# Local attention in blocks of 32 queries with 44 keys, its softmax in single operations, and coarse queries averaged on TensorE

## The chip, the cores and the metric

The kernel runs on one core of one Trainium2 chip. The metric is device microseconds of one launch: 507.03 us is the median of three runs before the change (505.02 to 508.1). One execution was taken by the hardware profiler; every row shown below is of that one.

## The reference, cut to what matters

There are 2 batches, 8 heads, 576 positions and a head width of 64. For each batch and head the kernel computes two attentions and adds them; the sum, transposed to 1152 tokens by 512, goes through two feed-forward layers (512 to 2048 to 512).

```python
# coarse attention: means of 4 positions, 144 queries by 144 keys
q_d, k_d, v_d = (t.reshape(B, H, 144, 4, D).mean(axis=3) for t in (q, k, v))
out_up = np.repeat(softmax(scale * q_d @ k_d.T) @ v_d, 4, axis=2)
# local attention: a key counts only where |query - key| < 4
scores = np.where(abs(pos[:, None] - pos[None, :]) < 4, scale * q @ k.T, -1e9)
out_local = softmax(scores) @ v
x = out_up + out_local          # -> (1152, 512)
# layer 1: h = x @ w_in;  g = P(h) / Q(h), polynomials;  x = g @ w_out
# layer 2: h = x @ w_in2; g = h * tanh(softplus(h));     out = g @ w_out2
```

The weights arrive as 64-bit floats and are turned into pairs of 32-bit values on ScalarE and VectorE. Each product of the layers is three matmuls (high by high, high by low, low by high).

## The kernel before, in words

**Planner.** The body adds tasks (`add`), each with its engines, the time it is believed to take on each, a priority, the tasks it follows and the buffers it takes. `Plan.run` walks a model of the time and emits the tasks of each of five queues (TensorE, ScalarE, VectorE, GpSimd, SyncE) in the order in which they start in that model; on the chip every queue then runs in that fixed order. A task that names two engines goes to the one that the model finds sooner, with a preference for the first named. Where TensorE has nothing ready before the model's 450 us it emits a filler matmul (`warm0`, `warm`, lines 442 and 445), whose result nobody reads.

**Attention units.** Sixteen units each take one batch, one pair of heads and 256 positions (4 windows of 64 queries); two mixed units take the last 64 positions of all four pairs of heads. So there are 18. Two heads lie on partitions 0 to 63 and 64 to 127. `prep` (eight times, once for each batch and pair) loads and transposes the keys and makes the coarse keys `kd` and coarse values `vd`. A unit then goes through these steps:

- `qload` (line 564) loads the queries, `vload` (line 578) the values of the 4 windows, 80 keys each, in two loads, one for each head.
- `pe_a` transposes the queries with 2 transposes (line 465) into a PSUM half bank `half`. From it `red` (line 599, VectorE) sums groups of four queries, `qscale` (line 616, GpSimd) scales the sums, and `qcopy` (line 609, ScalarE) copies the scaled queries to `qT`.
- `pe_b` writes a mask of -1e9 with 2 matmuls (line 638), adds the scores of 4 windows by 80 keys for each head (line 644), then the coarse scores by 144 keys (line 650). An f32 matmul stands as two instructions in the trace, so the 8 of line 644 are 16.
- `mx` takes the row maxima (lines 662 and 663, VectorE). `ex` runs four exponentials of 80 columns, each with its own bias and a read of its row sum (line 669), and one of 144 columns (line 673). `rc` makes the reciprocals of the sums (lines 681 and 684), `ns` scales the local part (line 689, GpSimd) and `npd` the coarse part (line 695, VectorE).
- `pe_d` transposes both parts (lines 707 and 711: 2 and 4 transposes); `copy_pd` (line 723) and `copy_p` (line 728) bring them from PSUM.
- `pe_e` multiplies by the values (lines 744 and 750). `od_c` (763) and `xadd` (770) add both attentions; `xhi` (789) and `xlo` (794) split the sum in two for the layers.

**Layers.** Layer 1 runs first over 6 of its 16 blocks of 128 hidden columns, in token chunks of 256, 256, 256 and 384; chunk c can start only when the units of its tokens are through. So units and layer 1 are interleaved on all engines until all units are done. The rest of layer 1, then layer 2, run in chunks of 384. Lines 1019 and 1167 are the matmuls of layer 1 (line 1019 also the first of layer 2), line 1169 those of the end of layer 2. Lines 899 to 930 turn the weights into pairs, lines 1040 to 1134 are the nonlinear parts.

**PSUM.** Two half banks `half` serve the query transposes and the coarse transposes in turn; scores, transposes `pt` and outputs `po` have one bank each. For the first chunk there is a second slot of each but `po`.

**Loads.** All loads are issued by SyncE in one order; a load that waits for its buffer holds those behind it.

## Time and profile before

| what | before |
|---|---|
| median of 3 runs | 507.03 us (505.02 to 508.1) |
| profiled execution, first to last instruction (span) | 502.4 us |
| median less the profiled span | 4.6 us |
| TensorE matmuls busy | 483.9 us, 96% |
| VectorE busy | 346.9 us, 69% |
| ScalarE busy | 341.7 us, 68% |
| GpSimd busy | 69.4 us, 14% |
| granted TensorE clock | 1.000 over the span |
| DMA | 44119 packets, 46.49 MB, 27568 packets under 512 B |

The profiled execution's own time is known only as its span; what lies around the span is taken as the 4.6 us to the median. PE stands for TensorE, PEld for its weight loads, DVE for VectorE, ACT for ScalarE, POOL for GpSimd and SP for SyncE; a q behind a name is its instruction queue. The busy shares are means over stages: the kernel has a stage with attention, one in which layer 1 runs alone, and one in which layer 2 runs alone.

### The profile page before, as it was taken

How to read it: one execution, taken by the hardware profiler on the slowest of the kernel's cores; microseconds unless marked ns; L12 is line 12 of the kernel's file. 1: busy time of each engine (PE TensorE's matmuls, PEld its weight loads, DVE VectorE, ACT ScalarE, POOL GpSimd, SP SyncE). 2: the span in 40 equal slices, each digit the busy share in tenths (PEclk: the TensorE clock that was granted, in tenths of full speed). 3: DMA queues.
4: the chain of work that ended last, by engine and by line, in shares of the span. 5: the costliest groups of instructions: out<-in, count | busy, mean ns of one | idle time of the engine just before them, and what ended most of it. 6: DMA issues, size and time to landing. Idle time of an engine off the chain costs nothing.

```text
span 502.4 us, 8614 instructions
## 1 busy us (share of the span) xinstructions
PE 483.9 (96%) x3468; PEld 442.0 (88%) x3468; DVE 346.9 (69%) x482; ACT 341.7 (68%) x612; POOL 69.4 (14%) x85
## 2 busy tenths in 40 slices
PE   8989898999999999999999989999999999999996
PEld 4568677899999999998998989899899899988995
DVE  5678888998999987989889999644723613222222
ACT  6699989998999999997999997555621322112210
POOL 3743764132000000000000413000000000000000
PEclk9999999999999999999999999999999999999999
DMA  9979765330245042315024040522400000000111
GB/s 186 208 226 199 205 176 145 105 105 14 87 166 168 2 168 83 90 78 168 2 83 168 8 161 1 167 85 83 168 0 1 0 1 0 1 0 1 63 64 63
DMA packets 44119, 46.49 MB, mean 93 GB/s; under 512 B 27568, under 2 KB 30640, under 8 KB 44080
## 3 DMA queue, kind: packets, MB, share of 16 engines
q1 hardware_dynamic: 44080, 45.95, 31.6%
q8 instruction: 27, 0.44, 0.4%
q14 instruction: 12, 0.10, 0.1%
HBM read 43.58 MB, written 2.36 MB: 91 GB/s over the span
## 4 chain that ended last, share of the span: by engine, by line
PE 45%; ACT 29%; DVE 13%; DMA 6%; issue 4%; SPq 1%; POOL 0%; DVEq 0%; ACTq 0%; POOLq 0%
PE psum L1019 21%; PE psum L1169 19%; ACT L961 4%; ACT raw L906 3%; DMA raw<-in_moe_w_in_dram 2%; ACT wt L899 2%; ACT wrk L1045 2%; PE psum L1167 2%; ACT late_f L1048 2%; ACT wrk L1040 2%; ACT late_f L977 2%; ACT att L669 1%; ACT gg L1134 1%; DMA att<-in_q_dram 1%; DVE wt L913 1%
## 5 line engine op out<-in xcount | busy, mean ns | idle before, releaser
L1019 PE MATMUL psum<-xh,wi 128*128 128x384 f32 (+1 forms) x528 | 132.5, 324 | 0.0
L1019 PEld LDWEIGHTS psum<-xh,wi 128*128 128x128 f32 x528 | 93.5, 188 | 1.2 <-issue 0.8
L1019 PE MATMUL psum<-xl,wi 128*128 128x384 f32 (+1 forms) x264 | 84.5, 320 | 0.0
L1019 PE MATMUL psum<-xh,late_r 128*128 128x384 f32 x288 | 76.7, 335 | 1.3 <-DVE late_f L1063 1.3
L1167 PE MATMUL psum<-gg,wo 128*128 128x384 f32 (+1 forms) x456 | 72.2, 312 | 0.9 <-ACT gg L1134 0.5
L1167 PEld LDWEIGHTS psum<-gg,wo 128*128 128x128 f32 x456 | 68.7, 189 | 2.3 <-ACT gg L1134 1.0
L1019 PEld LDWEIGHTS psum<-xh,late_r 128*128 128x128 f32 x288 | 52.3, 188 | 2.1 <-DVE late_f L1063 1.6
L1169 PE MATMUL psum<-wo,gg 128*128 128x512 f32 x216 | 51.1, 391 | 0.0
L1019 PEld LDWEIGHTS psum<-xl,wi 128*128 128x128 f32 x264 | 49.8, 189 | 0.2
L1019 PE MATMUL psum<-xl,late_r 128*128 128x384 f32 x144 | 48.3, 335 | 0.8 <-POOL xl L1226 0.8
L1169 PEld LDWEIGHTS psum<-wo,gg 128*128 128x128 f32 x216 | 40.4, 188 | 8.1
L1113 ACT ACTIVATE late_f<-psum 128x768 f32<-128x768 f32 (+1 forms) x12 | 9.5, 791 | 55.1 <-PE psum L1019 55.1
L913 DVE SCALAR_TENSOR_TENSOR wt<-wt,raw 128x1024 int32<-128x1024 int32 x32 | 41.7, 1304 | 5.0 <-ACT raw L906 4.1
L1246 DVE TENSOR_TENSOR part<-psum,part 128x512 f32<-128x512 f32 x27 | 18.4, 692 | 35.2 <-PE psum L1169 35.2
L899 ACT ACTIVATE wt<-raw 128x1024 f32<-128x1024 f32 x32 | 36.8, 1150 | 8.2 <-DVE late_r L930 3.8
L906 ACT ACTIVATE raw<-raw 128x1024 int32<-128x1024 uint16 x32 | 37.2, 1162 | 6.3 <-DMA raw<-in_moe_w_out_dram 4.7
L1113 ACT ACTIVATE wrk<-psum 128x768 f32<-128x768 f32 (+1 forms) x13 | 10.3, 790 | 43.2 <-PE psum L1019 43.2
L1226 POOL TENSOR_TENSOR xl<-part,xh 128x768 fp32r<-128x768 f32 x5 | 11.6, 2321 | 176.5 <-ACT xh L1221 176.0
L1139 DVE TENSOR_TENSOR gg<-wrk,gg 128x768 fp32r<-128x768 f32 (+1 forms) x22 | 18.6, 845 | 23.1 <-ACT gg L1113 22.9
L1019 PEld LDWEIGHTS psum<-xl,late_r 128*128 128x128 f32 x144 | 27.0, 188 | 1.4 <-POOL xl L1226 1.1
L1169 PE MATMUL psum<-wo,late_r 128*128 128x512 f32 x108 | 25.7, 391 | 0.0
L1139 DVE TENSOR_TENSOR gg<-late_f,gg 128x768 fp32r<-128x768 f32 (+1 forms) x15 | 15.4, 1024 | 14.4 <-ACT gg L1113 13.9
(135 smaller groups left out, 937.7 us busy)
## 6 DMA issues: line engine op xcount, KB each, us to landing
raw<-in_moe_w_in_dram SPq DMA_DIRECT2D x16, 1024.0 KB, 5.2
raw<-in_moe_w_out_dram SPq DMA_DIRECT2D x16, 1024.0 KB
att<-in_v_dram SPq DMA_DIRECT2D x36, 80.0 KB, 5.0
out_dram<-part SPq DMA_DIRECT2D x9, 256.0 KB, 2.2
att<-in_q_dram SPq DMA_DIRECT2D x16, 128.0 KB, 4.0
att<-in_k_dram SPq DMA_DIRECT2D x6, 288.0 KB, 4.4
att<-in_v_dram SPq DMA_DIRECT2D x6, 256.0 KB, 4.0
wrk<-in_k_dram SPq DMA_DIRECT2D x2, 288.0 KB, 5.8
```

The lines of the kernel that those rows point to most:

```text
L899: nc.scalar.activation(out=t.v, in_=words(r)[:, :, 1].bitcast(F32), func=AF.Prelu if fold else AF.Identity, scale=2.0 ** -112, **({"alpha" ...
L906: nc.scalar.activation(out=words(r)[:, :, 0], in_=r.v.bitcast(U16).rearrange("p (n four) -> p n four", four=4)[:, :, 1], func=AF.Copy, sca ...
L913: nc.vector.scalar_tensor_tensor(out=ti, in0=ti, scalar=3, in1=words(r)[:, :, 0], op0=ALU.logical_shift_left, op1=ALU.bitwise_or)
L961: nc.scalar.preload_act_table_set(name)
L977: nc.scalar.activation(out=st.B(), in_=st.B(), func=AF.Sigmoid, scale=-1.0)
L1019: nc.tensor.matmul(st.h.v[:, i, :T], w.v[:, ww, ks], xx[:, kk, c0:c0 + T], start=(nn == 0 and (st.big or i == 0)), stop=(nn == 3 * KD - 1 ...
L1113: nc.scalar.activation(out=vw(dst), in_=H(), func=AF.Mish)
L1139: ENG[e].tensor_tensor(out=vw(st.gl), in0=vw(st.c), in1=vw(st.gh).bitcast(F32), op=ALU.subtract)
L1167: nc.tensor.matmul(A(d)[:, :T], w.v[:, ww, lo + d * 128:lo + (d + 1) * 128], vw(gg)[:, i, :], start=start, stop=stop)
L1169: nc.tensor.matmul(A(d), vw(gg)[:, i, sl], w.v[:, ww, lo:lo + DM], start=start, stop=stop)
L1226: ENG[e].tensor_tensor(out=xl[xs], in0=pv, in1=xh[xs].bitcast(F32), op=ALU.subtract)
L1246: nc.vector.tensor_tensor(out=pv, in0=acc.v[:, j], in1=pv, op=ALU.add)
```

## The change

The windows of a unit become blocks of 32 queries with 44 keys (`WK` 80 to 44), eight to a unit. Their results lie in a `[128, 4, 44]` array of scores: partition quarters hold head and block, and `SLOT` gives the place of a window.

- `vload` issues four loads of 44 keys in place of two of 80 (eight small ones for a mixed unit), and values of two windows lie on partitions 0 to 43 and 64 to 107.
- `pe_a` writes the transposed queries interleaved and averages the coarse queries with two matmuls against `mean`; `red` and `qscale` are gone, and one `qcopy` of 320 columns takes both.
- `pe_b` has one mask matmul over all partitions and 16 of 44 columns in place of 8 of 80.
- After `mx`, `below` subtracts the maxima on VectorE, `ex` is one exponential over 176 columns, and `rc` begins with a row sum on VectorE. `npd` moves to GpSimd; its factor 0.25 moves to `od_c`.
- `pe_d` transposes two blocks at once (2 and 2 transposes, all into `pt`); `copy_p` copies twice 256 columns on one engine, and `copy_pd` is gone.
- `pe_e` has 16 products of 32 columns in place of 8 of 64.
- The query transposes have one PSUM slot `q_s` (two in the first chunk) and the products one slot `px_s`. The masks come from one band copied by VectorE, and the filler multiplies zeros in `blank`.

```diff
--- before.py
+++ after.py
...
-    WK, WS = 80, 61
+    WK, HB = 44, 32
...
+    eye2 = const.tile([64, 128], BF16, name="eye2")
+    mask = const.tile([64, 11, WK], BF16, name="mask")
+    band = const.tile([64, 88], BF16, name="band")
+    blank = const.tile([128, 480], BF16, name="blank")
+    mean = const.tile([128, 64], F32, name="mean")
...
-    qT_s = lay("att", 2, 256, (4, 64))
-    qd_s = lay("att", 2, 64)
+    qT_s = lay("att", 2, 320)
...
+    vw_s = lay("att", NVW, 512, (4, 2, D), parts=64 + WK)
+    s_s = lay("att", 2, 256, (4, 64))
...
+    pT_s = lay("att", 2, 512, parts=64 + WK)
...
-    half_s = [bank(8 + i, 9 + i, psum[:, 4, 256 * i:256 * i + 256]) for i in range(2)]
+    q_s = [bank(8, 9.25, psum[:, 4, :320])]
+    px_s = [bank(9.25, 10, psum[:, 4:8:3, 320:448])]
...
+    MASK0, SLOT = (0, 3, 7), (0, 2, 1, 3)
+
+    def window(i, w, b):
+        if i == 0 and w < 2:
+            return 29 * (2 * w + b)
+        return min(64 * w + HB * b - 3, S - WK)
...
+        for s in tm_s + qx_s + s_s:
             nc.vector.memset(mem["att"][:, s.lo:s.hi], 0.0)
+
+    def means():
+        nc.vector.tensor_reduce(
+            out=mean, in_=ident.rearrange("p (s two) -> p s two", two=2), axis=AX.X, op=ALU.add
+        )
+        nc.vector.tensor_scalar(out=mean, in0=mean, scalar1=1.0 / 16.0, scalar2=None, op0=ALU.mult)
...
+        nc.tensor.matmul(view[:, :480], blank[:, :128], blank, start=True, stop=True)
+
+    t_bl = add({"dve": 0.25}, lambda: nc.vector.memset(blank, 0.0), -2000)
+    plan.filler = (warm_s + sc_s + pt_s + po_s, ((t_bl, warm),), 0.19)
...
+            for w0, nb in ((0, 4), (2, 4)) if not mixed else [(w, 2) for w in range(4)]:
+                p, (k0, k1) = keys[w0]
+                for hh in range(2):
+                    src = v[bb, 2 * p + hh]
+                    nc.sync.dma_start(
+                        out=vw.v[64 * (w0 // 2):64 * (w0 // 2) + WK, 2 * (w0 % 2):2 * (w0 % 2) + nb, hh, :],
+                        in_=bass.AP(src.tensor, src.offset + k0 * D, [[D, WK], [(k1 - k0) * D, nb], [1, D]]),
+                    )
...
+            q2 = qp.v[:, :2 * n].rearrange("c (p r) -> c p r", r=2)
             for r in range(2):
-                flip(half.v[:, r * n:(r + 1) * n], qn.v, r, n)
-
-        ta = add(
-            {"pe": 0.16 + 0.02 * nw}, pe_a, prio, after=[l0, t_id], take=[half, qT, qd], use=[qn], chain="pa"
-        )
-
-        def ps3():
-            return half.v[:, :2 * n].rearrange("c (r n) -> c r n", r=2)
-
-        def red():
-            nc.vector.tensor_reduce(
-                out=qt.v[:, :16 * nw], in_=ps3().rearrange("c r (s u) -> c s r u", u=2), axis=AX.XY, op=ALU.add
-            )
-
-        tr = add({"dve": t_dve(2 * n)}, red, prio, after=[ta], take=[qt], use=[half])
+                flip(q2[:, :, r], qn.v, r, n)
+            for r in range(2):
+                nc.tensor.matmul(
+                    qp.v[:, 2 * n:2 * n + 64], qn.v[:, 2 * D * r:2 * D * (r + 1)], mean, start=(r == 0), stop=(r == 1)
+                )
+
+        ta = add({"pe": 0.48}, pe_a, prio, after=[l0, t_id, t_mn], take=[qp, qT] + mix, use=[qn], chain="pa")
...
+            ops = [(qT.v, qp.v[:, :320])]
+            if mixed:
+                ops = [
+                    (qT.v[:, :256], qp.v[:, :256]),
+                    (qx.v[:, :, :16], qp.v[:, 256:320].rearrange("c (w s) -> c w s", w=4)),
+                ]
+            for dst, src in ops:
+                if e == "act":
+                    nc.scalar.activation(out=dst, in_=src, func=AF.Identity, scale=SCALE)
+                else:
+                    nc.vector.tensor_scalar(out=dst, in0=src, scalar1=SCALE, scalar2=None, op0=ALU.mult)
...
-            for h in hs:
-                nc.tensor.matmul(
-                    sc.v[h, :nw * WK], ident16[h, h], mask[h, m0:m0 + nw].rearrange("p w x -> p (w x)"),
-                    start=True, stop=False,
-                )
+            nc.tensor.matmul(
+                sc.v[:, :nw * WK], eye2, mask[:, m0:m0 + nw].rearrange("p w x -> p (w x)"), start=True, stop=False,
+            )
             for w in range(nw):
-                for h in hs:
-                    nc.tensor.matmul(
-                        sl3()[h, w, :], qT.v[h, w], kT[keys[w][0]][h, keys[w][1]:keys[w][1] + WK],
-                        start=False, stop=(w == nw - 1),
-                    )
+                for b in range(2):
+                    for h in hs:
+                        r0, c0 = h.start + HB * b, 64 * w + HB * b
+                        nc.tensor.matmul(
+                            sl3()[r0:r0 + HB, SLOT[w], :], qT.v[h, c0:c0 + HB], kT[keys[w][0]][h, keys[w][1][b]:keys[w][1][b] + WK],
+                            start=False, stop=(w == nw - 1), tile_position=(h.start, r0),
+                        )
...
-        def ex():
-            for w in range(nw):
-                nc.scalar.activation(
-                    out=s.v[:, w], in_=sl3()[:, w], func=AF.Exp, bias=tm.v[:, w:w + 1],
-                    accum_out=tm.v[:, 5 + w:6 + w],
-                )
+        def sv():
+            return s.v[:, :, :WK]
+
+        def below():
+            nc.vector.tensor_tensor(
+                out=sv(), in0=sl3(), in1=tm.v[:, 0:nw].unsqueeze(2).to_broadcast([128, nw, WK]), op=ALU.add
+            )
+
+        tl = add({"dve": t_dve(WK * nw)}, below, prio, after=[tx], use=[sc, tm, s])
+
+        def ex_d():
             nc.scalar.activation(
                 out=pd.v, in_=sd2(), func=AF.Exp, bias=tm.v[:, 4:5],
                 accum_out=tm.v[:, 9:10],
             )
 
-        te = add({"act": 0.36 + 0.296 * nw}, ex, prio, after=[tx], use=[sc, tm, s, pd])
+        te_d = add({"act": 0.53}, ex_d, prio, after=[tx], use=[sc, tm, pd])
+
+        def ex():
+            nc.scalar.activation(out=sv(), in_=sv(), func=AF.Exp)
+
+        te = add({"act": t_act(WK * nw)}, ex, prio, after=[tl], use=[s])
 
         def rc():
+            nc.vector.tensor_reduce(out=tm.v[:, 5:5 + nw], in_=sv(), axis=AX.X, op=ALU.add)
             nc.vector.tensor_scalar(
                 out=tm.v[:, 10:15], in0=tm.v[:, 5:10], scalar1=1e-9, scalar2=None, op0=ALU.add
             )
             nc.vector.reciprocal(out=tm.v[:, 10:15], in_=tm.v[:, 10:15])
 
-        tc_ = add({"dve": 0.35}, rc, prio, after=[te], use=[tm])
+        tc_ = add({"dve": 0.35 + t_dve(WK * nw)}, rc, prio, after=[te, te_d], use=[tm, s])
...
+            nc.gpsimd.tensor_scalar(
+                out=pd.v, in0=pd.v, scalar1=tm.v[:, 14:15], scalar2=1.0, op0=ALU.mult, op1=ALU.mult,
...
             add({"pool": t_pool(WK * nw), "dve": t_dve(WK * nw)}, ns, prio, after=[tc_], use=[tm, s], port=True),
-            add({"dve": 0.2}, npd, prio, after=[tc_], use=[tm, pd], port=True),
+            add({"pool": 0.3}, npd, prio, after=[tc_], use=[tm, pd]),
...
+            for j in range(2):
+                nc.tensor.transpose(
+                    pt.v[:64 + WK, j * 128:(j + 1) * 128],
+                    s.v[:, 2 * j:2 * j + 2].rearrange("p w x -> p (w x)")[:, :64 + WK], ident,
+                )
             for t in range(2):
                 nc.tensor.transpose(
-                    half2.v[:72, t * 128:(t + 1) * 128], pd.v[:, t * 72:(t + 1) * 72], ident
-                )
-            for w in range(nw):
-                nc.tensor.transpose(pt.v[:WK, w * 128:(w + 1) * 128], s.v[:, w, :], ident)
-
-        td = add(
-            {"pe": 0.32 + 0.11 * nw}, pe_d, prio, after=tn, take=[half2, pt, pT, pdT], use=[s, pd], chain="pd"
-        )
-
-        def copy_pd(e):
-            dst = pdT.v.rearrange("c t h x -> c (t h) x")[:, :, :16 * nw]
-            src = half2.v[:72, :256].rearrange("c (a x) -> c a x", a=4)[:, :, :16 * nw]
-            if e == "act":
-                nc.scalar.activation(out=dst, in_=src, func=AF.Identity)
-            else:
-                nc.vector.tensor_copy(out=dst, in_=src)
+                    pt.v[:72, 256 + t * 128:256 + (t + 1) * 128], pd.v[:, t * 72:(t + 1) * 72], ident
+                )
+
+        td = add({"pe": 0.5}, pe_d, prio, after=tn, take=[pt, pT], use=[s, pd], chain="pd")
...
+            for rows, lo, hi in ((64 + WK, 0, 256), (72, 256, 512)):
+                dst, src = pT.v[:rows, lo:hi], pt.v[:rows, lo:hi]
+                if e == "act":
+                    nc.scalar.activation(out=dst, in_=src, func=AF.Identity)
+                else:
+                    nc.vector.tensor_copy(out=dst, in_=src)
 
         tp = [
-            add({"dve": t_dve(2 * n), "act": t_act(2 * n, True)}, copy_pd, prio, after=[td], use=[half2, pdT]),
-            add({"act": t_act(nw * 128, True), "dve": t_dve(nw * 128)}, copy_p, prio, after=[td], use=[pt, pT]),
+            add({"act": t_act(256, True) * 2, "dve": t_dve(256) * 2}, copy_p, prio, after=[td], use=[pt, pT]),
...
+                for b in range(2):
+                    for hh, h in enumerate(hs):
+                        r, c = slice(64 * (w // 2), 64 * (w // 2) + WK), 128 * (w % 2) + 64 * hh + HB * b
+                        nc.tensor.matmul(
+                            px.v[h, w // 2, 64 * (w % 2) + HB * b:64 * (w % 2) + HB * b + HB], vw.v[r, 2 * (w % 2) + b, hh, :], pT.v[r, c:c + HB],
+                            start=True, stop=True,
+                        )
...
+                out=xt.v.rearrange("c (a s f) -> c a s f", a=2, f=4),
+                in0=px.v.rearrange("c a (s f) -> c a s f", f=4),
+                in1=od.v.rearrange("c (a s) -> c a s", a=2).unsqueeze(3).to_broadcast([128, 2, 32, 4]), op=ALU.add,
...
```

## Rows read from the trace of the kernel before

**Rows 1.** the page's 40 slices: busy tenths of PE, ACT and DMA
```profile
PE   8989898999999999999999989999999999999996
ACT  6699989998999999997999997555621322112210
DMA  9979765330245042315024040522400000000111
```

**Rows 2.** windows: us, busy (x count) of PE, PEld, DVE, ACT, POOL, clock, DMA
```profile
0.00:100.00 100.00, 89.86 (x1126) 69.97 (x1127) 80.56 (x180) 85.00 (x271) 49.46 (x71) 1.00 0.76 182
100.00:215.00 115.00, 115.00 (x887) 113.25 (x886) 106.73 (x140) 110.50 (x172) 8.40 (x9) 1.00 0.31 101
215.00:305.00 90.00, 85.50 (x482) 82.94 (x481) 81.71 (x81) 84.31 (x95) 9.38 (x4) 1.00 0.26 88
```

**Rows 3.** chain of waits to 130 us: start us, length us, what
```profile
17.11 7.38 DMA raw<-in_moe_w_in_dram
52.46 7.14 DMA att<-in_q_dram
65.20 1.23 ACT att L669 x8
```

**Rows 4.** ACT timeline: start us, length us; spacings are differences of starts
```profile
64.61 0.60 ACT L728 ACTIVATE att<-psum 80x512 f32<-80x512 f32 x1
65.08 0.33 ACT L669 ACTIVATE att<-psum,att 128x80 f32<-128x80 f32 x1
67.15 0.39 ACT L609 ACTIVATE att<-psum 128x256 f32<-128x256 f32 x1
67.41 1.18 ACT L906 ACTIVATE raw<-raw 128x1024 int32<-128x1024 uint16 x1
```

**Rows 5.** groups by form, DVE and one of POOL: total us, mean ns, idle
```profile
L599 DVE TENSOR_REDUCE att<-psum 128x64 f32<-128x256 f32 x18 | 7.3, 412 | 1.1 <-PE psum L707 0.5 <-PE psum L465 0.2 <-ACT att L609 0.2
L695 DVE TENSOR_SCALAR att<-att 128x144 f32<-128x144 f32 x18 | 10.9, 608 | 0.0
L723 DVE COPY att<-psum 72x256 f32<-72x256 f32 x18 | 7.4, 410 | 1.2 <-ACT att L609 1.2
L662 DVE TENSOR_REDUCE att<-psum 128x4 f32<-128x320 f32 x18 | 8.6, 475 | 2.5 <-PE psum L650 2.2
L770 DVE TENSOR_TENSOR att<-psum,att 128x256 f32<-128x256 f32 x18 | 7.5, 418 | 4.7 <-ACT att L763 3.9 <-POOL xl L794 0.7
L1055 DVE TENSOR_TENSOR wrk<-wrk,psum 128x512 f32<-128x512 f32 x9 | 6.1, 682 | 1.3 <-ACT wrk L1048 0.8 <-ACT wrk L1045 0.5
L689 POOL TENSOR_TENSOR att<-att 128x320 f32<-128x320 f32 x17 | 14.4, 849 | 7.3 <-DVE att L684 3.5 <-ACT att L728 3.5 <-ACT wrk L1078 0.4
```

**Rows 6.** chain of waits, parts of units on PE
```profile
105.18 0.25 PE psum L638 x2
105.43 0.55 PE psum L644 x16
112.11 0.47 PE psum L750 x16
107.72 0.44 PE psum L711 x4
```

**Rows 7.** PE timeline: products of 16 columns, then of 64
```profile
121.07 1.11 PE L744 MATMUL psum<-att 72*64 72x16 f32 x32
122.02 0.67 PE L750 MATMUL psum<-att 80*64 80x64 f32 x16
```

**Rows 8.** windows to 100 us of lines 445, 644 and 750 alone, PE
```profile
0.00:100.00 100.00, 16.45 (x64) 1.00 0.76 182
0.00:100.00 100.00, 11.58 (x256) 1.00 0.76 182
0.00:100.00 100.00, 8.99 (x224) 1.00 0.76 182
```

**Rows 9.** line 578, loads of values: SyncE issue ns, min/median/max
```profile
L578 SPq DMA_DIRECT2D att<-in_v_dram x36: 312/412/2055, 9.4 to 113.0; - x36
```

More of the change, by code (lines that the diff above doesn't have):

```diff
@@ L374 @@
     early = {
-        "half": [bank(i, i + 1, psum[:, 0, 256 * i:256 * i + 256]) for i in range(2)],
+        "q": [bank(0, 2, psum[:, 0, :320])],
         "s": [bank(2, 4, psum[:, 1])], "pt": [bank(4, 6, psum[:, 2])], "po": [],
@@ L620, in qds @@
-        def qds(i):
-            return qd.v.rearrange("c w x -> c (w x)")[:, 64 * i:64 * i + 64] if mixed else qd.v
-        tq = [
-            add({"act": t_act(2 * n, True), "dve": t_dve(2 * n)}, qcopy, prio, after=[ta], use=[half, qT]),
-            add({"pool": 0.22}, qscale, prio, after=[tr, t_cd], use=[qt, qd]),
-        ]
+                flip(q2[:, :, r], qn.v, r, n)
[3 more added lines that the diff above has]
+                )
@@ L628, in sl3 @@
+        def qds(i):
+            return qx.v.rearrange("c w x -> c (w x)")[:, 64 * i:64 * i + 64] if mixed else qT.v[:, 256:320]
+        ex_ = 0.2 if mixed else 0
+        tq = add({"act": t_act(320, True) + ex_, "dve": t_dve(320) + ex_}, qcopy, prio, after=[ta, t_cd], use=[qp, qT] + mix)
         def sl3():
@@ L652, in unit @@
         tb = add(
-            {"pe": 1.3 if mixed else 0.84}, pe_b, prio,
-            after=tq + [kv_done[p] for p in pairs] + [t_i16, t_mk[0 if m0 == 0 else 1]],
+            {"pe": 1.4 if mixed else 0.95}, pe_b, prio,
+            after=[tq] + [kv_done[p] for p in pairs] + [t_i16, t_mk[kind]],
             take=[sc, tm, s, pd],
-            use=[qT, qd], chain="pb",
+            use=[qT] + mix, chain="pb",
         )
@@ L748, in pe_e @@
             for w in range(nw):
[L749 to L753 removed]
+                for b in range(2):
+                    for hh, h in enumerate(hs):
[3 more added lines that the diff above has]
+                            start=True, stop=True,
+                        )
         tf = add(
[L756 to L757 removed]
+            {"pe": 1.2 if mixed else 0.87}, pe_e, prio, after=tp + [vl] + [vd_done[p] for p in pairs], take=[po, px, od, xt],
+            use=[vw, pT], chain="pe",
         )
@@ L763, in od_c @@
             nc.scalar.activation(
-                out=od.v[:, :16 * nw], in_=po.v[:, 256:256 + 16 * nw], func=AF.Identity
+                out=od.v[:, :16 * nw], in_=po.v[:, :16 * nw], func=AF.Identity, scale=0.25
             )
```

125 lines of the change are left out of this document (34 added, 91 removed).

## The prediction

> **What bounds the kernel now.** I read the page's slices first [rows 1]. After slice 24 (some 305 us) ScalarE is mostly idle and TensorE is full to the end: that is layer 2, which the change doesn't touch. Ahead of that both are nearly full, so a mean over the kernel says nothing; the windows by stage do [rows 2].
>
> From 215 to 305 us TensorE is busy 85.5 of 90 us: 4.5 us are lost while ScalarE, busy 84.31, is late. From 100 to 215 us TensorE is busy 115.00 of 115 us. From 0 to 100 us no engine is full: ScalarE 85.00, VectorE 80.56, TensorE 89.86, of which 16.45 are the 64 fillers of line 445, that do nothing useful [rows 2, 8]. So TensorE has 73.4 us of work there. The 256 instructions of line 644 and 224 of line 750 [rows 8], at 16 a unit, say that 16 units have their scores and 14 their outputs by 100 us. This stage is what the change can shorten; every microsecond taken from it moves the TensorE-bound rest forward.
>
> The chain of waits names what holds this stage: trains of exponentials (eight records, 1.23 us), and loads: a first weight load of 7.38 us, a query load of 7.14 us [rows 3].
>
> **The change part by part.**
>
> *ScalarE.* The train of four exponentials takes 1.23 us [rows 3]; one exponential of 176 columns takes its place. A PSUM copy of 512 columns spaces the next start by 65.08 - 64.61 = 0.47 us, one of 256 by 67.41 - 67.15 = 0.26 us [rows 4], so 0.82 ns a column. At that rate 176 columns take 0.26 - 0.07 = 0.19 us; the upper end is a quarter of the train, 0.31, plus 96 columns, 0.39. I take 0.24, nearer the copies, since bias and sum read go. That is -0.99 us a unit. Two copies of 256 take 0.52 in place of 0.47 (+0.05), and `qcopy` is 64 columns longer (+0.05). Together -0.89, with ends of -0.74 and -0.94: for 16 units -14.2 us, for all 18 -16.
>
> *VectorE.* The sum of line 599 (0.412), the scaling of line 695 (0.608) and the copy of line 723 (0.410) go; the maximum of line 662 loses 144 columns [rows 5]. A column costs (682 - 418)/256 = 1.03 ns [rows 5], so that is -0.15. Subtraction and row sum come at 418 - 80 x 1.03 = 336 ns each. The sum is -0.91 us a unit, or -0.24 if the planner puts both 256-column copies on VectorE. I take -0.85: some -13 us for 16 units.
>
> *GpSimd.* Line 689 took 0.849 us for 320 columns [rows 5]; for 176 between 0.47 (by columns) and 0.85. The coarse scaling comes behind it on the same queue, 0.38 to 0.85 by the same row, and `qscale` goes. GpSimd is busy 49.46 of 100 us [rows 2], so the total is covered; but `pe_d` waits for both, and behind them are queued `xlo` and the sums of coarse values. The two in a row take about what the longer one took before; I count nothing, at the worst 0.8 us on a unit's way, covered while other units are under way.
>
> *TensorE.* The scores go from 16 to 32 instructions, the products with the values from 16 to 32. What does one cost at half the columns? The trace has a row: 32 products of 16 columns take 122.02 - 121.07 = 0.95 us [rows 7], 29.7 ns each, as much as one of 64 columns, 0.47/16 = 29.4 [rows 6]. So halving columns does not halve time, and I take 29.7: scores 0.55 to 0.95 (+0.40), products 0.47 to 0.95 (+0.48). By columns alone they would be +0.06 and 0; that is the other end. The Trainium skill, "TensorE: Matmul & The Clock Gate", section "Wait — 56ns, not 53.3ns?", gives a floor of some 25 ns from start to start however few the columns. By that both would take 0.80, an estimate, and the increase would be 0.58 and not 0.88; the measured row decides.
>
> The mask falls from 0.25 [rows 6] to some 0.10 (-0.15). Two transposes fewer are -0.22, as four take 0.44 [rows 6]. The two averaging matmuls are four instructions: 29.7 ns each if they are like the small ones (0.12), 0.11 each if like a transpose (0.44); with half the columns of a transpose I take 0.22. Together +0.73 a unit, with ends of -0.19 and +0.92. Up to 100 us that is some +11 us (16 units of scores, 14 of outputs): 73.4 becomes 84 us. Fillers give way to it, since the planner puts them only where nothing is ready.
>
> *What the first stage becomes.* ScalarE 85 - 14 = 71, VectorE 80.6 - 13 = 67.6, TensorE 84. The busiest useful engine covers 85% of the stage now. TensorE cannot fill it wholly, the first queries have to come; if it covers 95% the stage takes 88 us, if 85%, 99 us. I take 92, so -8 us: the relief of both other engines makes up more than the extra work, as they are the ones on the chain. A unit's own way is also shorter: 1.23 goes, 0.24 + 2 x 0.34 comes.
>
> *Behind it.* After 100 us TensorE has no slack, and two units' scores and four units' outputs are still to come: 2 x 0.25 + 4 x 0.48 - 4 x 0.22 = +1.5 us. ScalarE is relieved by 16 us in all and TensorE moves forward by some 6.5, so part of the 4.5 us of lost time comes back: I take -2, between 0 and -4.5.
>
> *Loads.* A non-mixed unit issues four value loads for two, at a median of 412 ns each [rows 9]: +0.82 us of SyncE a unit, 13 us for 16 units, and 704 packets of 256 bytes for 640. Queued behind them are queries and weights. SyncE is not full, but in the first slices the DMA engines are [rows 1], and the first weights are on the chain [rows 3]. Here the ends are 0 and +13; I take +1.5, nearer 0, since four units' loads at most stand ahead of the first weights. Constants (masks, `mean`, two more memsets) cost nothing as long as the first queries and keys are still on their way.
>
> The sum is -8 + 1.5 - 2 + 1.5 = -7 us. Against the profiled execution, span 502.4 us, that is 495.4; with the 4.6 us around it 500.0, against the median of 507.03 us.
>
> **The rivals.**
>
> *A, the forecast,* 495 to 505 us, chance 0.53.
>
> *B, TensorE's extra work is small* (price by columns, -0.19 a unit). Then TensorE has some 70 us and ScalarE's 71 us bind, at a cover of 85% in 84 us: -16, -2 behind, +1.5 for loads, some 490 us. Against it speaks the row of 16 columns. Chance 0.12.
>
> *C, the gain is eaten.* At +0.92 a unit TensorE has 87 us in a stage where fillers and gaps were, and at a cover of 90% it takes 97 us: -3, +2 behind, no stall returned, +1.5 for loads: 0.5 us longer, 507.5, with 504 to 510 around it. The same comes out if the new planned order fits the chip worse, or ScalarE's relief falls in gaps where it waited for loads anyway. For it: 73.4 is already large and the loads on the chain don't shrink. Chance 0.25.
>
> *D, the value loads hold up the rest; slower.* SyncE issues in order; each unit holds it 0.82 us longer, and what stands behind (queries of the next unit, weights) starts later by as much. If all of it lands on the chain, 500 + 13 - 1.5 = 511.5, and with longer landings some 513 us. It decides from the point where more than 7 us of the 13 are exposed. For it: the query load that took 7.14 us [rows 3]; against it, that the DMA share falls after the first slices [rows 1]. Chance 0.10. The Trainium skill, "DMA: Bandwidth & Descriptors", section "Why a DMA increments its semaphore by 16 and not by 1", has a rule against this change: a load runs on the largest number of engines, up to 16, that divides its slowest dimensions, so 80 keys would use 16 and 44 keys 11. The busiest engine would then carry 1.6 times as much of the values, an estimate. No row of this trace shows how many engines a load uses.
>
> **How the numbers follow.** The time is A's, 500 us. The range of 490 to 508 holds A, the upper half of B and most of C, some 0.83 of the chance. What this kernel's measurement can tell from no change is about 1%, so faster means under 502, slower over 512. Faster: three quarters of A, all of B, a little of C, 0.54. Slower: most of D and the tail of C, 0.11. Same: 0.35.
>
> **What would show it.** Of the profile of the changed kernel: one exponential of 176 columns near 0.24 us of spacing, and ScalarE 14 us lighter ahead of the point where 16 units have scores; 32 score instructions in some 0.95 us (B: 0.6); fillers fewer than 64; the start of layer 2's full stretch some 7 us ahead of 305; the stall before it 2 to 3 us; the first weight load landing within 3 us of 24.5. The forecast is wrong if TensorE waits for queries or weights in the first 60 us for longer than now, if the units end later although ScalarE is lighter, or if the granted clock, 1.00 in every window [rows 2], falls.

## The result: slower, and the profile after

The changed kernel takes 513.09 us, the median of 4 runs, against 506.11 us for the kernel before in the same rounds: ratio 1.0143, 95% interval 1.011 to 1.0175. I had forecast 500.0 us, with 490 to 508. The profiled execution spans 512.1 us, against 502.4. Medians are of all executions, ratios leave out the few far slower ones (of the kernel called "more fillers" below, one took 805.61 us).

The two profiles lie 9.7 us apart, the medians 7.0. What lies around the span is 1.8 us in the four executions of the changed kernel and about 2 us in those of the kernel before in later rounds, not the 4.6 us that I took. So the profiled execution of the kernel before, some 504.4 us by this estimate, was a quick one.

The slices (PE, granted clock, DMA busy tenths) have the old shape; the windows have the columns of [rows 2].

```profile
PE   9998998999999999999999989999999999999996
PEclk9999999899999999999999999999999999999999
DMA  8769687310504231452224022432400000000111
```

```profile
0.00:100.00 100.00, 91.39 (x1502) 72.68 (x1503) 65.05 (x168) 71.49 (x174) 39.62 (x60) 0.98 0.74 183
100.00:215.00 115.00, 111.80 (x1012) 107.73 (x1012) 102.58 (x142) 99.33 (x151) 10.38 (x14) 1.00 0.28 89
215.00:305.00 90.00, 86.36 (x489) 84.12 (x488) 81.99 (x84) 85.13 (x94) 5.57 (x2) 1.00 0.28 94
...
88.00:92.00 4.00, 3.47 (x24) 3.13 (x24) 3.32 (x7) 2.93 (x5) 2.78 (x4) 0.61 0.30 74
```

To be seen: up to 100 us ScalarE fell from 85.00 to 71.49 and VectorE from 80.56 to 65.05 [rows 2], close to what I had put down (71 and 67.6), and no time came of it. A part of the fall is work not yet reached: by 100 us 15 units have their scores and 13 their outputs, where the kernel before had 16 and 14. Between 100 and 215 us TensorE now has 3.2 us of gaps where it had none. One slice has a lower clock: 0.61 from 88 to 92 us.

Here are the changed groups by form (ns of one, then idle time ahead and who ended it), answering to [rows 5].

```profile
L700 POOL TENSOR_SCALAR att<-att 128x144 f32<-128x144 f32 x18 | 10.2, 568 | 0.0
...
L695 POOL TENSOR_TENSOR att<-att 128x176 f32<-128x176 f32 x17 | 9.2, 540 | 30.3 <-DVE att L690 15.4 <-ACT xh L788 4.4 <-ACT att L762 2.7
...
L769 DVE TENSOR_TENSOR att<-psum,att 128x256 f32<-128x256 f32 x18 | 7.6, 424 | 19.3 <-PE psum L716 6.4 <-PE psum L645 6.3 <-PE psum L598 4.1
...
L681 ACT ACTIVATE att<-att 128x176 f32<-128x176 f32 x18 | 6.3, 351 | 1.4 <-DVE att L666 1.3
...
L666 DVE TENSOR_TENSOR att<-psum,att 128x176 f32<-128x176 f32 x18 | 6.0, 335 | 3.1 <-ACT att L673 3.1
L686 DVE TENSOR_REDUCE att<-att 128x4 f32<-128x176 f32 x18 | 5.9, 330 | 2.4 <-ACT att L681 2.3
```

The odd one is line 769, the final addition: 19.3 us of waiting, where line 770 had 4.7 [rows 5], ended by lines 716, 645 and 598. It reads none of their results. They are coarse transposes, coarse scores and averages of other units, which write banks 6, 5 and 4; its view takes banks 4 and 7 in one step. TensorE is held in turn: its transposes wait for this addition (total, times, longest).

```profile
PE psum L711 <- DVE att L769: 3.3, 6, 0.7
```

TensorE's parts of a unit (start, length of a run of matmuls), answering to [rows 6]:

```profile
67.28 0.25 PE L632 MATMUL psum<-mask,eye 64*128 64x176 bf16 x1
67.46 0.52 PE L639 MATMUL psum<-att 64*32 64x44 f32 x32
67.91 0.46 PE L645 MATMUL psum<-att 64*64 64x144 f32 x4
...
69.77 0.56 PE L598 MATMUL psum<-mean,att 128*128 128x64 f32 x4
70.13 0.37 PE L1018 MATMUL psum<-xh,wi 128*128 128x256 f32 x1
...
71.40 0.92 PE L749 MATMUL psum<-att 44*64 44x32 f32 x32
72.26 0.47 PE L474 MATMUL psum<-ident,att 96*128 96x96 f32 x3
```

From start to next start, the 32 instructions of the scores take 0.45 us, the 32 of the products 0.86, the averages 0.36.

**Where the 9.5 us are.** The slowdown is complete when layer 2 is in full stretch. The 1322nd matmul of the layers starts at 312.9 us (303.4 before); what remains takes 199.2 us (199.0). I split TensorE's time up to it, from its first matmul on, each matmul counted up to the next one's start or its own end. All rows are of single, profiled executions, so by the medians some 2.5 of the 9.5 us are scatter. "Half" is the time up to six us before the end at a granted clock of 0.50, that is 1.2 GHz in place of 2.4; it overlaps the other columns.

```
kernel                         1322nd  attention  layers  fillers  idle   half
before                          303.4     58.4     212.7    18.0   13.1    0
after                           312.9     70.2     215.9    11.4   14.3    3.4
before, more TensorE work       308.6     70.1     212.1    17.8    7.4    0
before, one exponential         303.9     59.7     213.9    18.9   10.3    6.8
before, short fillers           309.1     65.3     213.6     6.3   22.7   13.6
after, light TensorE            313.4     64.3     217.6    12.4   17.9   27.3
after, third buffer, two adds   307.2     70.8     214.6    11.2    9.3   13.6
the same, light TensorE         303.2     59.2     215.8    10.8   16.3   10.2
```

TensorE's attention grew by 11.8 us, fillers gave back 6.6, layers grew by 3.2 (1.0 of it in twelve matmuls at half clock, shown below; the rest no run explains), idle time by 1.2. In a stage with so much more work on TensorE, idle time should have shrunk; the kernel before with the same work added shows by how much (7.4).

### The profile page after: what moved, and what is told of

Same layout as the page of the kernel before. It is cut to its first block, busy times and chain, and to the rows that moved or that the text cites. A ratio compares the mean times of both kernels' runs of the same rounds, so it can differ in the third digit from the quotient of the medians.

```text
span 512.1 us, 9690 instructions
## 1 busy us (share of the span) xinstructions
PE 492.2 (96%) x4028; PEld 449.1 (88%) x4028; DVE 336.5 (66%) x481; ACT 327.1 (64%) x506; POOL 61.6 (12%) x79
## 4 chain that ended last, share of the span: by engine, by line
PE 53%; ACT 23%; DVE 15%; DMA 4%; issue 3%; POOL 1%; SPq 0%; DVEq 0%; ACTq 0%; POOLq 0%
PE psum L1018 19%; PE psum L1168 19%; ACT L960 3%; ACT raw L905 2%; PE psum L749 2%; PE psum L1166 2%; ACT wt L898 2%; ACT wrk L1044 2%; PE psum L474 2%; DMA raw<-in_moe_w_in_dram 2%; PE psum L456 2%; ACT late_f L1047 1%; PE psum L645 1%; DMA raw<-in_moe_w_out_dram 1%; ACT wrk L1039 1%
## 5 line engine op out<-in xcount | busy, mean ns | idle before, releaser
L1166 PE MATMUL psum<-gg,wo 128*128 128x384 f32 (+1 forms) x456 | 74.3, 316 | 1.8 <-DVE gg L1138 1.8
L1166 PEld LDWEIGHTS psum<-gg,wo 128*128 128x128 f32 x456 | 69.8, 192 | 3.3 <-DVE gg L1138 2.8
L1225 POOL TENSOR_TENSOR xl<-part,xh 128x768 fp32r<-128x768 f32 x5 | 11.6, 2320 | 179.1 <-ACT xh L1220 178.5
L1138 DVE TENSOR_TENSOR gg<-late_f,gg 128x768 fp32r<-128x768 f32 (+1 forms) x15 | 15.4, 1027 | 14.3 <-ACT gg L1112 13.9
```

The source lines that it names most:

```text
L1138: ENG[e].tensor_tensor(out=vw(st.gl), in0=vw(st.c), in1=vw(st.gh).bitcast(F32), op=ALU.subtract)
L1166: nc.tensor.matmul(A(d)[:, :T], w.v[:, ww, lo + d * 128:lo + (d + 1) * 128], vw(gg)[:, i, :], start=start, stop=stop)
L1225: ENG[e].tensor_tensor(out=xl[xs], in0=pv, in1=xh[xs].bitcast(F32), op=ALU.subtract)
```

## The experiments

P: TensorE's added work decides. W: waits between engines and the written order decide. S: ScalarE's relief shortens the stage (my forecast's step). L: late value loads. C: TensorE's clock.

| kernel | median, us | before, us | ratio, 95% | granted clock |
|---|---|---|---|---|
| two adds | 511.66 | 505.30 | 1.0115 (1.0076 to 1.0153) | 0.980 to 0.996 |
| loads of 48 rows | 518.22 | 505.30 | 1.0218 (1.0129 to 1.0308) | 0.977 to 0.997 |
| averages on VectorE | 521.75 | 505.30 | 1.0293 (1.0215 to 1.0371) | 0.977 to 0.990 |
| coarse exponential later | 518.71 | 505.30 | 1.0255 (1.0172 to 1.0338) | 0.974 to 0.986 |
| more fillers | 517.25 | 505.44 | 1.0201 (1.0139 to 1.0263) | 0.987 to 0.997, one 0.555 |
| measured costs | 530.63 | 505.44 | 1.0505 (1.0429 to 1.058) | 0.958 to 0.976 |
| light TensorE | 511.83 | 505.44 | 1.0154 (1.0107 to 1.0202) | 0.972 to 0.990 |
| before, one exponential | 503.89 | 505.44 | 0.9964 (0.9925 to 1.0003) | 0.990 to 1.000 |
| before, more TensorE work | 510.59 | 505.39 | 1.0095 (1.0064 to 1.0127) | 0.992 to 1.000 |
| light TensorE, dense matmuls | 515.41 | 505.39 | 1.0179 (1.0128 to 1.0229) | 0.993 to 1.000 |
| before, softmax alone | 521.19 | 505.39 | 1.0308 (1.0248 to 1.0368) | 0.979 to 0.992 |
| third buffer | 511.76 | 506.21 | 1.0087 (1.0048 to 1.0126) | 0.983 to 0.993 |
| third buffer, two adds | 508.96 | 506.21 | 1.0058 (1.0022 to 1.0093) | 0.983 to 0.993 |
| the same, light TensorE | 506.75 | 506.21 | 1.0021 (0.9976 to 1.0066) | 0.973 to 0.990 |
| before, short fillers | 508.18 | 506.21 | 1.0037 (1.0003 to 1.007) | 0.979 to 0.989 |

The last column is the granted clock, mean over an execution, from the lowest to the highest execution. Within one kernel the time goes with it: of the 31 executions of the kernel before that were made beside the last four kernels, nine at 0.998 to 1.000 span 501.4 to 503.3 us, six at 0.989 to 0.991 span 504.7 to 508.4. At 0.995 to 0.997 the other 16 span 502.3 to 505.9, and the changed kernel's four 510.5 to 513.1. So the loss is there at the same clock too, and theory C does not explain it.

The cuts below give long lines in words.

**Two adds.** The final addition once for each bank.

```diff
-  out=xt.v.rearrange("c (a s f) -> c a s f", a=2, f=4), in0=px.v.rearrange("c a (s f) -> c a s f", f=4), ...
+  for g in range(2):
+      out=xt.v[:, 128 * g:128 * g + 128]..., in0=px.v[:, g]..., in1=od.v[:, 32 * g:32 * g + 32]...
```

> The changed kernel with one edit: the sum of both attentions is two adds, one for each PSUM bank, in place of one add whose view strides over banks 4 and 7. Theory W (the strided view makes that add wait for the scores and transposes of the next unit, which it does not read, and makes them wait for it): VectorE's idle time ahead of the add falls from 19.3 us to under 8, TensorE's transposes no longer wait for it (3.3 us before), the time falls by 5 to 12 us, to 501 to 508 against 513. Theory P (TensorE's and GpSimd's extra work is the cost): within 2 us of 513. Theory L (value loads on the queue of loads): within 2 us of 513.

The interval overlaps that of the changed kernel. The wait shrank, though:

```profile
L770 DVE TENSOR_TENSOR att<-psum,att 128x128 f32<-128x128 f32 x36 | 8.8, 285 | 9.7 <-PE psum L598 4.5 <-ACT att L762 4.4 <-ACT att L613 0.8
```

Lines 716 and 645 (banks 6 and 5) no longer lead it, and TensorE's transposes and matmuls no longer wait for it (two weight loads do, 0.5 us together); line 598 writes bank 4, where half of the products still lie. So the wide view made the first two waits, but alone they are a small part of the loss. A lower clock hides some of the gain: the three executions at 0.995 and 0.996 span 508.1 to 508.9 us, the changed kernel's four 510.5 to 513.1. The Trainium skill, "PSUM — Partial Sum Buffer", section "PSUM bank collisions raise a hardware error", wants two engines' accesses ordered by bank and not by address; the wait on line 598 agrees with it, those on banks 5 and 6 go beyond it. Both halves in one bank was not tried.

**Loads of 48 rows, averages on VectorE, coarse exponential later.** Three edits of the changed kernel: four more keys in each value load; the averages back on VectorE and GpSimd; `ex_d` made to follow the subtraction. In the last two the planner's order moved with the edit (62 and 52 fillers for 38).

```diff
-  DMA rows [D, WK]                       # 44
+  DMA rows [D, 48]
---
-  two matmuls against mean, one qcopy of 320 columns
+  tensor_reduce on VectorE, tensor_scalar on GpSimd, qcopy of 256
---
-  te_d = add({"act": 0.53}, ex_d, prio, after=[tx], ...)
+  te_d = add({"act": 0.53}, ex_d, prio, after=[tl], ...)
```

> The changed kernel with the value loads of the sixteen plain units 48 keys long in place of 44, of which 44 are used as before; same number of loads, 9% more bytes. Theory L with the rule that a load runs on the largest number of engines up to 16 that divides its rows (44 on 11, 48 on 16): loads land sooner, the time falls by 2 to 8 us. Theories W and P: within 1.5 us of 513.

> The changed kernel with the coarse queries summed on VectorE and scaled on GpSimd again, as before the change, in place of the two matmuls on TensorE. Theory P: TensorE loses 0.4 us a unit, 7 us in all, and the time falls by 3 to 7 us. Theory W: the waits stay, within 2 us of 513, since VectorE and GpSimd get 0.33 and 0.24 us a unit back. Theory L: within 2 us of 513.

> The changed kernel with the coarse exponential put behind the subtraction of the maxima: both read the bank of the scores, and in the changed kernel the subtraction waits for the coarse exponential in 12 of 18 units. Theory W, widened to any two instructions on one PSUM bank: a unit's way is up to 0.4 us shorter, the time falls by 0 to 4 us. Theories P and L: within 1.5 us of 513.

All three were slower than the changed kernel, and no theory had that. In each TensorE ran at 0.50 for longer: 20.5, 13.6 and 13.6 us against 3.4. So these medians cannot price their edits. One execution with 48 rows had the changed kernel's clock, 0.997, and spans 513.9 us: nothing shows of the 2 to 8 us that L expected. The runs made me look at what stood ahead of each fall, here in the changed kernel (TensorE, timeline):

```profile
84.64 1.71 PE L1166 MATMUL psum<-gg,wo 128*128 128x256 f32 x12
86.49 0.43 PE L711 MATMUL psum<-ident,att 128*108 128x128 f32 x2
88.53 0.41 PE L716 MATMUL psum<-ident,att 128*72 128x128 f32 x2 [1.61 <-POOL att L700]
88.70 2.73 PE L1166 MATMUL psum<-gg,wo 128*128 128x256 f32 x12
```

A wait of 1.61 us, then twelve matmuls in 2.73 us that had taken 1.71. The chain tells why TensorE waited (start, length):

```profile
78.31 6.18 DMA att<-in_v_dram
84.68 1.32 POOL att L543
86.00 0.44 POOL att L695
86.44 0.86 POOL xl L793
87.30 1.19 POOL att L700
```

The coarse scaling (line 700), which the change moved to GpSimd, stands in GpSimd's queue behind a value sum that a load held up, and behind line 793; TensorE's transpose waits for it.

**More fillers, measured costs.** Only the written order changes: 77 fillers for 38; or the planner's costs of `pe_a`, `pe_e` and `npd` set to what the trace shows.

```diff
-  FILL = 0.5
+  FILL = 0.8
---
-  pe_a 0.48;  pe_e 1.2 if mixed else 0.87;  npd 0.3
+  pe_a 0.60;  pe_e 1.9 if mixed else 1.24;  npd 0.45
```

> The changed kernel with the planner's bound for fillers raised from 0.5 to 0.8, which puts 77 fillers into the order in place of 38; nothing else. Theory C (the changed kernel's loss is TensorE's clock: it was granted 0.50 for 3.4 us behind 88.9, where fillers had become few, and nothing before) expects no stretch at 0.50 and 509 to 511 us. Theory P (TensorE itself has become the engine that the first 130 us wait for: its time in attention lines is 70.2 us against 58.4, and fillers then cost what they take) expects 515 us or more: some 39 fillers of 0.2 us more, less what falls in idle time. If fillers lie in idle time only, the time stays at 511 to 514.

> The changed kernel with three of the planner's costs set to what the trace of the changed kernel shows (transposes and averages of the queries 0.60 for 0.48, products of a unit 1.24 for 0.87 and 1.90 for 1.20 where a unit is mixed, GpSimd's scaling of the coarse weights 0.45 for 0.30), so that only the written order of the instructions changes. Theory W (the order is what is wrong: instructions are queued for times that the engines cannot keep, and each late one holds what is queued behind it) expects 503 to 509 us and values that lag the plan by less than 28 us at the last unit. Theory P (TensorE's own work decides) expects at best 510 to 513 us, since the work is the same.

Theory C falls as put: twice the fillers left 13.6 us at 0.50, behind new waits (one of 1.85 us on line 769), and cost 8 us of TensorE. W's hope of a better order falls too: with truer costs the order left 44.4 us at 0.50. The work is the same, so order alone, with the clock that fell with it, moved the time by 17.5 us. How much of the change's own loss is its new order, no run separates.

**Light TensorE**, in the same order.

```diff
-  16 products of 32 columns, each with its block's keys; averages r = 0 and 1
+   8 products of 64 columns with the first block's keys; averages r = 0 alone
```

> The changed kernel in the same written order, with less work on TensorE alone: the products of a window take both blocks of queries with the first block's keys (16 instructions a unit for 32), and the averages leave out the second half of the query heads (2 for 4), so attention's time on TensorE falls by about (0.40 + 0.20) x 18 = 11 us, to what it was before. The output is another one. Theory P (TensorE's added work decides) expects 501 to 505 us, 8 to 12 below the changed kernel. Theory W (waits between the engines and the order decide) expects 510 to 513 us, TensorE idle for the difference. In between, 506 to 509, both have a part.

Neither: the time is the changed kernel's, but TensorE was not idle for the difference. Windows of 4 us (columns as above) and the wait in the first of them:

```profile
24.00:28.00 4.00, 2.44 (x32) 2.15 (x29) 0.86 (x5) 1.65 (x4) 0.84 (x2) 0.76 0.62 137
28.00:32.00 4.00, 4.00 (x35) 2.43 (x33) 2.50 (x6) 2.51 (x8) 1.43 (x1) 0.50 0.64 163
...
40.00:44.00 4.00, 4.00 (x46) 3.60 (x44) 0.92 (x1) 1.48 (x6) 0.00 (x0) 0.61 1.01 262
44.00:48.00 4.00, 3.83 (x77) 3.06 (x65) 2.65 (x8) 2.72 (x8) 1.91 (x3) 1.00 1.12 276
```

```profile
26.08 1.33 PE L745 MATMUL psum<-att 44*64 44x64 f32 x16 [1.56 <-DMA att<-in_v_dram]
```

Behind one wait of 1.56 us on values, TensorE is busy 4.00 of 4 us at 0.50 for 17 us, and for 10 us more behind 91. The work that was taken out came back as slower work: attention is only 5.9 us below the changed kernel's and idle time 3.6 above. This profile has the lowest clock of the four executions, 0.972; the others, at 0.986 to 0.990, span 509.2 to 510.2 us.

**Before, one exponential**, in the same order.

```diff
-  for w in range(4): exp(sl3()[:, w], bias=tm.v[:, w:w + 1], accum_out=...)
+  exp(sl3(), bias=tm.v[:, 0:1], accum_out=tm.v[:, 5:6])
```

> The kernel before in the same written order, with less work on ScalarE alone: the four exponentials of a unit's windows are one operation (the first window's maximum for all, one sum), some 0.85 us less of ScalarE in each of 18 units, 15 us in all, and nothing added on any engine. The output is another one. Theory S, my forecast's first step (ScalarE's relief shortens the first stage by 8 us), expects 497 to 500 us against 506. Theories P and W (ScalarE is not what the first stage waits for) expect 503 to 507.

S falls. Up to 100 us ScalarE loses 10 us [rows 2] and nothing else gets shorter:

```profile
0.00:100.00 100.00, 92.52 (x1121) 71.87 (x1122) 81.40 (x179) 75.03 (x180) 49.45 (x71) 0.97 0.75 181
```

The gain is 0.4% with an interval that touches none. The profiled execution had 6.8 us at 0.50, which hides 3.4 us at the most; four executions at 0.999 and 1.000 span 499.5 to 501.6, five of the kernel before 502.2 to 503.4. So the relief of ScalarE alone is worth some 2 us, not 8.

**Before, more TensorE work**, in the same order.

```diff
-  8 products of 64 columns;  2 query transposes
+  16 products of 32 columns; the 2 query transposes made twice
```

> The kernel before in the same written order, with more work on TensorE alone: the products of a window in two halves of 32 queries (32 instructions a unit for 16, as the changed kernel has them) and the transposes of the queries made twice; together some (0.38 + 0.25) x 18 = 11 us more, about what attention's lines take more on TensorE in the changed kernel (70.2 us against 58.4). The result is the same. Theory P (TensorE's added work decides) expects 511 to 516 us. Theory W (waits in the new chain and order of the changed kernel decide, and a stage in which TensorE runs 18 us of fillers absorbs such work) expects 504 to 508.

The span is 507.8, 5.4 us longer for 11.7 us more in attention; idle time took 5.7. The clock stayed at 1.00. So nearly half of the added work reaches the end, a little under what P expected. By the medians it is 5.2 us, three quarters of the 7.0 that the change lost. The first 100 us:

```profile
0.00:100.00 100.00, 95.36 (x1311) 77.09 (x1312) 77.39 (x174) 82.74 (x267) 46.86 (x68) 1.00 0.75 178
```

**Light TensorE, dense matmuls.** Two matmuls of 128 by 128 by 256 added to each lightened unit.

```diff
+  if w % 2 == 0: matmul(po.v[:, 64:320], blank[:, :128], blank[:, :256])
```

> The changed kernel lightened on TensorE as before (16 products a unit with the first block's keys, half of the averages), in the same order, with two matmuls of 128 by 128 by 256 added to each unit's products, whose result nobody reads: 0.2 us of full-width work for some 0.6 us of narrow work that was taken out. The output is another one. The lightened kernel without them had TensorE at 0.50 for 17 us behind 26 and for 10 us behind 91, and took 511.8 us. If that half clock is what gave the lightened work back, and the full-width work prevents it, 502 to 507 us and less than 7 us at 0.50. If TensorE's work was not what the changed kernel waits for, 510 to 513 whatever the clock.

Inconclusive: half clock fell to 3.4 us, but the 36 dense matmuls took 0.43 us a unit where I had put down 0.2, and the products between them grew from 8.9 to 14.1 us in all, so attention stood at 70.8 us again, and the time with it.

**Before, softmax alone.**

```diff
-  four exponentials with bias and row sum
+  subtraction on VectorE, one exponential, row sum on VectorE (80 keys)
```

> One part of the change alone in the kernel before: the softmax in single operations per unit (VectorE subtracts the maxima, one exponential, VectorE sums the rows), still with 80 keys, 64 queries to a block and the queries averaged on VectorE. ScalarE some 0.7 us lighter a unit, VectorE some 0.8 us heavier, TensorE's work the same. Theory P (TensorE decides) expects 504 to 508 us as long as the clock stays at 1.00. Theory W (the longer chain of a unit between VectorE and ScalarE delays the units) expects 509 to 514. My forecast's view (the engine with the most busy time decides, and here VectorE takes ScalarE's place) expects 506 to 510.

Slower than every theory had it. The planner's order is another one (89 fillers for 72). TensorE's attention is unchanged (58.4 us), VectorE is busy 87.87 of the first 100 us for 80.56 [rows 2], and new waits stand in layer 1, two of them with a fall to 0.50 behind it, here the first:

```profile
194.47 0.45 PE L1027 MATMUL psum<-xh,late_r 128*128 128x384 f32 x1 [2.74 <-ACT late_f L1056]
```

**Third buffer; third buffer and two adds; the same with light TensorE; before with short fillers.**

```diff
-  NKN, NVW, NXT, NQN = 2, 2, 3, 3
+  NKN, NVW, NXT, NQN = 2, 3, 3, 3
---
-  the 72 fillers of the kernel before: 480 columns
+  128 columns (8 of them) and 80 columns (64)
```

> The changed kernel with three buffers for a unit's values in place of two, so that their loads do not stand in SP's queue until the products two units earlier are done (26.5 us of such waits in the changed kernel), nor the queries and values queued behind them. The written order moves a little (37 fillers for 38). Theory L (late loads hold the units back) expects 505 to 509 us and no TensorE wait on a load or on GpSimd's value sums above 1 us in the first 100 us. Theory P (TensorE's work, with waits of other kinds) expects 510 to 514.

> Both: the third buffer for values, and the final addition of a unit as two operations of one bank each in place of one view over two banks (alone that gave 511.7 us and 508.3 in its profile). If the two waits are separate and both count, 502 to 506 us. If one takes the place of the other, or TensorE's work decides, 508 to 512.

> Both of these, and TensorE lightened by 11 us as before (16 products a unit with the first block's keys, half of the averages; the output is another one). Lightened alone it had a 1.56 us wait on values before it ran at 0.50 for 17 us, and one of 1.61 us on GpSimd before 10 us more, and took 511.8. If the half clock behind such waits is what gave the lightened work back, fewer of them give 497 to 503 us. If TensorE's work is not on the path at all, the same time as the kernel with both and the full work.

> The kernel before in the same written order and with the same 72 fillers, each of 128 or 80 columns for 480: some 12 us less of filler time on TensorE, nothing else. If fillers stand only in idle time and keep the clock, their shortening costs clock: stretches at 0.50 and 508 to 515 us. If they take TensorE's time from the work behind them, as the added work did (5.2 us of 12 came through), and the clock stays at 1.00, 499 to 502 us.

L alone misses its 505 to 509. With both waits treated the time falls to 508.96, an interval that no longer overlaps the changed kernel's; TensorE's idle time falls from 14.3 to 9.3 us with the same work. With light TensorE on top 506.75: attention 11.6 us shorter, the 1322nd matmul 4.0 us earlier. That interval overlaps the one without it. TensorE's attention is then near the kernel before's (59.2 for 58.4), both waits are treated, ScalarE and VectorE are relieved, and the time is the kernel before's, at a lower clock. Four executions at 0.986 to 0.990 span 501.6 to 507.8 us, the six of the kernel before at 0.989 to 0.991 504.7 to 508.4: at the same clock a little of the relief may show. Windows up to 100 us, of the first and the second of these two:

```profile
0.00:100.00 100.00, 95.40 (x1587) 76.76 (x1589) 73.40 (x194) 78.29 (x190) 43.60 (x64) 0.95 0.77 186
```

```profile
0.00:100.00 100.00, 88.98 (x1359) 70.26 (x1360) 73.14 (x195) 77.83 (x191) 43.49 (x64) 0.95 0.76 186
```

Short fillers made the kernel before no faster: 11.7 us of fillers less, 9.6 us of idle time more, 13.6 us at 0.50. Its ten executions have a clock of 0.979 to 0.989, and none of 31 of the kernel before was below 0.989. So the kernel's fillers stood in idle time and kept the clock:

```profile
0.00:100.00 100.00, 80.07 (x1039) 68.49 (x1040) 76.44 (x169) 80.18 (x254) 46.38 (x68) 0.93 0.74 170
```

No version of the changed kernel beat the kernel before.

## Why the prediction was wrong

**The step that failed is "what the first stage becomes", the -8 us.** I took the busiest engine's useful share as what sets the stage, and said that the relief of ScalarE and VectorE "makes up more than the extra work, as they are the ones on the chain". The relief came: over all units' own lines, each instruction counted up to the next one's start, ScalarE lost 0.72 us a unit (I had 0.89, at least 0.74) and VectorE 0.98 (I had 0.85). But ScalarE's alone, in the kernel before, is worth 1.5 us (0.9964, interval touching 1); VectorE's alone was not tried. The work that I covered with it, TensorE's, costs 5.2 us when it is added alone. An engine with 85 of 100 us and a place on the chain was not the limit: every engine waits in order, and of added TensorE work about half finds idle time.

**ScalarE's and VectorE's terms** were near: a new exponential takes 0.24 to 0.26 us where the next instruction follows at once. That 71.49 and 65.05 us came so close is in part luck, as a unit's work less lies in them.

**"Behind it"** was wrong: TensorE loses 3.2 us between 100 and 215 us, where it had no gap, and the idle time in the 90 us ahead of layer 2's full stretch fell only from 4.5 to 4.0 us, where I had 2 to 3.

**TensorE's term** was right in sum and wrong in parts. I had +0.73 us a unit, +13 in all; attention grew by 11.8, 0.66 a unit. (Its parts add up to +0.95 at the upper end, not +0.92.) Scores cost 0.45 us where I took 0.95, 14 ns each and not 29.7 [rows 7]; products 0.86, near it, 27 ns. The floor of 25 ns, which I cited from the Trainium skill, "TensorE: Matmul & The Clock Gate", section "Wait — 56ns, not 53.3ns?", agrees with the products; the scores, which use quarters of the array (64 by 32), lie below it. Averages were dearer (0.36 to 0.44 for 0.22), and the masks no cheaper (3.2 us in all, 2.8 before), where I had 0.15 a unit off.

**GpSimd at nothing, at worst 0.8 us a unit covered by other units,** stood ahead of the one fall of the clock in the profile: line 700 behind a value sum that had waited 6.18 us for its load.

**Waits that I had not priced:** the addition's view over two banks. With it and the value buffer treated, 0.85% of the 1.43% is gone; how much of this belongs to which stays open, since single intervals overlap and a third buffer moves the order a little. SyncE waited 26.5 us for value buffers up to 130 us, but 26.1 in the kernel before too (line 578 behind line 750, 11 times each), so the held queue itself is not new. The rows of SyncE (total, times, longest), before and after:

```profile
SPq L578 <- PE psum L750: 26.1, 11, 6.6
SPq L586 <- PE psum L749: 26.5, 11, 5.5
```

Added up, 5.2 us for TensorE's work less 1.5 for ScalarE's relief leave 3.3 of the 7.0 for waits and order, and treating both waits took 4.1 off the median (513.09 to 508.96). This is an estimate: each of these figures is known to about 2 us, and the kernel with both waits treated ran at a lower clock.

**The rivals** of the prediction. C was the nearest mechanism (extra TensorE work in a stage where fillers and gaps were, an order that fits worse), with a price too low: 504 to 510. D named the time, 511.5 to 513, by loads, and met it more by luck: TensorE's matmuls waited for no load in the first 60 us (2.1 us before), and the third buffer, which frees SyncE's queue, gave back little. GpSimd's value sums did wait longer for their loads, 21.1 us for 13.0. Which engines a load of 44 keys uses, no run here shows.

**Of the signs I named,** the exponential, ScalarE's 14 us, fewer fillers (38 for 72) and the first weight load (first used at 26.9 us, 2.4 later) came; the scores in 0.95 us did not (0.45). Layer 2's full stretch came 9.5 us later where I had 7 earlier; units end later though ScalarE is lighter (the last addition starts at 129.5 us, 123.6 before), and the granted clock fell, as the forecast's own list of failures had it. The last sign says little, as other executions of the kernel before go down to 0.989.

Not settled: why single parts of the change alone (softmax, averages undone) are worse than the whole by more than their time at 0.50 explains.

## What to carry to other kernels

Where all engines run in a fixed order and none is full, a relief counts only if work alone on that engine can be shown to move the end: lighten one engine in the same order and look, before adding work to another. Work on the engine that bounds the later stages cost about half of itself here, even where there were gaps and fillers. Before a buffer is given a view over several PSUM banks, look at who else writes to any bank between its ends. Compare kernels at the same granted clock: one kernel's executions differed by up to 7 us here.

## What the runs showed of the hardware

- In 15 of the 17 kernels' profiled executions the granted clock fell to 0.50 (1.2 GHz) before their last microseconds. Ahead of each of those falls TensorE had waited, the longest time between 0.58 and 3.6 us; the kernel before has a wait of 1.30 us with no fall, "before, softmax alone" one of 2.92 us, at 88 us. The cost is not the wait: 17 us at half clock stood behind 1.56 us.
- An instruction of an f32 matmul with 64 by 32 weights and 44 columns, on a quarter of the array, starts every 14 ns (32 in 0.45 us), one with 44 by 64 weights and 32 columns every 27 ns (32 in 0.86 us).
- The row sum over 176 columns took 330 ns, the subtraction from PSUM 335 ns; GpSimd needed 568 ns for 144 columns by one scalar, where VectorE had needed 608 [rows 5].
